# One DMA in place of two for three stores at the end of an attention and MLP kernel

## The chip, the cores and the metric

The kernel runs on one core of one Trainium2 chip. The metric is device time in microseconds; a run of the kernel before takes 364.1 us (median of three runs, 363.9 to 364.14). The names of the engines are those of the profile: PE is TensorE, PEld its weight loads, DVE is VectorE, ACT is ScalarE, POOL is GpSimd, SP is SyncE. SP, ACT and POOL also issue DMAs, each on a queue of its own; the core has 16 DMA engines, which do the moving.

## What is computed

Attention with a sigmoid in place of the softmax, and behind it a two-layer MLP with SiLU on all tokens:

```python
# q, k, v: (8, 12, 448, 64); w_in: (768, 2048); w_out: (2048, 768)
scores = q @ k.T / sqrt(64) - log(448)
attn_out = sigmoid(scores) @ v
x = attn_out.transpose(0, 2, 1, 3).reshape(3584, 768)
h = x @ w_in
out = (h * sigmoid(h)) @ w_out          # (3584, 768), float32
```

## The kernel before

The inputs are cast to 16 bits when they are loaded. Attention, the first matrix product (h) and the second (out) are interleaved by hand: generators issue a few TensorE instructions at a time, and an outer loop takes turns between them. The batches are handled in four pairs, m = 0 to 3. For m = 0 to 2 the out products of one pair run between the attention work of the next; for the last pair nothing is left to run between, so the kernel ends with a plain stretch of out products (the loop at L830).

The tokens of a batch are cut into 64 rows of 7 neighbours: token p * 7 + c belongs to chunk c (0 to 6), row p (0 to 63). `rows_of` (L490) is this view of the output: `rows_of[b, c]` is a piece of 64 rows of 768 floats, whose rows lie 7 output rows apart. Chunks c and c + 1 of one batch are neighbouring output rows. On chip, two chunks make up one block of 128 partitions: the first 64 partitions hold the one, the next 64 the other. `row_blocks(m, g)` (L518) gives the two output pieces that belong to block g of pair m; the 14 chunks of a pair make 7 blocks. Blocks 0 to 2 and 4 to 6 lie within one batch, block 3 takes the last chunk of one batch and the first of the next.

`out_set` (L521 to L580) computes two blocks at once. It uses seven products in place of eight, each of 8 matrix instructions into one PSUM bank (`product`, L535), with sums and differences on VectorE before and after. The results are two tiles `osb` of 128 x 768 floats, one for each block, and each has a left and a right half of 384 columns: c11 and c12 of the first, c21 and c22 of the second. In all sets but the last, each block is stored whole, as two DMAs of 64 rows by 3,072 bytes on SP. In the last set (`last=True`) each half is stored as soon as it is there, in pieces of 64 rows by 1,536 bytes:

- L556, after the second product: left half of the first block (c11), two DMAs on SP
- L567, after the fifth product: left half of the second block (c21), one on SP, one on ACT
- L572, after the sixth product: right half of the second block (c22), two on SP
- L577, after the seventh product: right half of the first block (c12), one on SP, one on ACT

The VectorE instructions that complete these halves are L553 (c11), L565 (c21), L570 (c22) and L575 (c12). The last set pairs block 6 of pair m = 2 with block 6 of pair m = 3: each is made of chunks 5 and 6 of one batch (L617 to L621). A queue issues its DMAs in the order of the program; the instruction that issues waits for the data by semaphore, and what stands behind it on that queue waits too.

Of the kernel before, what the change touches and what calls it, by code (L numbers as in the profile page):

```python
# [17 lines left out]
def kernel(  # L18
# [9 lines left out]
    nc = tc.nc  # L28
# [5 lines left out]
    HP = P // 2  # L34
    NCH = S // HP
# [53 lines left out]
    def one_bank(name):  # L89
        if "any" in banks:  # L90
            ring.append(ring.pop(0))
            return banks["any"].tile([P, 512], F32, tag=f"any{ring[-1]}", name=name)
        taken["single"] += 1
        return banks["single"].tile([P, 512], F32, tag="single", name=name)
# [395 lines left out]
    rows_of = out.rearrange("(b p c) e -> b c p e", b=B, c=NCH)  # L490
# [25 lines left out]
        return gTr[:, :, at : at + P]  # L516

    def row_blocks(m, g):  # L518
        return [rows_of[2 * m + u // NCH, u % NCH] for u in (2 * g, 2 * g + 1)]

    def out_set(a1, rows1, a2, rows2, last=False):  # L521
        lo, hi = slice(0, NHC), slice(NHC, NFC)
        osb = [p3.tile([P, DMODEL], F32, tag="osb", name="osb") for _ in range(2)]
        c11, c12 = (osb[0][:, nh * NO2 : (nh + 1) * NO2] for nh in range(2))
        c21, c22 = (osb[1][:, nh * NO2 : (nh + 1) * NO2] for nh in range(2))
        m1 = cpool.tile([P, NO2], F32, tag="m1", name="m1")
        sg = [cpool.tile([P, NHC, P], F16, tag=f"S{i}", name=f"S{i}") for i in range(1, 5)]

        def store(rows, o, cols, engines):
            for at, (row, eng) in enumerate(zip(rows, engines)):  # L530
                eng.dma_start(row[:, cols], o[at * HP : (at + 1) * HP, cols])

        left, right, whole = slice(0, NO2), slice(NO2, DMODEL), slice(0, DMODEL)

        def product(a, w):  # L535
            po = one_bank("po")
            for fc in range(NHC):
                nc.tensor.matmul(  # L538
                    po[:, :NO2], a[:, fc, :], w[:, fc, :], start=(fc == 0), stop=(fc == NHC - 1)
                )  # L540
                if fc < NHC - 1:
                    yield 163
            return po[:, :NO2]

        add, sub = nc.vector.tensor_add, nc.vector.tensor_sub
        add(sg[0], a2[:, lo], a2[:, hi])
        sub(sg[1], sg[0], a1[:, lo])
        po = yield from product(a1[:, lo], wq[0][0])
        (act_copy if last else nc.vector.tensor_copy)(m1, po)
        sub(sg[2], a1[:, lo], a2[:, lo])  # L550
        yield 163
        po = yield from product(a1[:, hi], wq[1][0])
        add(c11, po, m1)  # L553
        sub(sg[3], a1[:, hi], sg[1])
        if last:
            store(rows1, osb[0], left, (nc.sync, nc.sync))  # L556
        yield 163
        po = yield from product(sg[1], tw[2])
        add(c12, po, m1)
        yield 163  # L560
        po = yield from product(sg[2], tw[3])
        add(c22, po, c12)
        yield 163
        po = yield from product(a2[:, hi], tw[4])
        sub(c21, c22, po)  # L565
        if last:
            store(rows2, osb[1], left, (nc.sync, nc.scalar))  # L567
        yield 163
        po = yield from product(sg[0], tw[1])
        add(c22, po, c22)  # L570
        add(c12, po, c12)
        store(rows2, osb[1], right if last else whole, (nc.sync, nc.sync))  # L572
        yield 163
        po = yield from product(sg[3], wq[1][1])
        add(c12, po, c12)  # L575
        if last:
            store(rows1, osb[0], right, (nc.sync, nc.scalar))  # L577
        else:
            store(rows1, osb[0], whole, (nc.sync, nc.sync))
        yield 163  # L580
# [25 lines left out]
    def sets(m):  # L606
        for g in range(0, NCH - 1, 2):
            step = out_set(
                block(m, g), row_blocks(m, g), block(m, g + 1), row_blocks(m, g + 1)
            )  # L610
            for i, ns in enumerate(step):
                if m == 0 and g == 0 and i in (10, 14):
                    next(sums)
                if m == 0 and g == 0 and i in (20, 28, 36, 44):
                    next(in_sums)
                yield ns
        if m % 2 == 1:  # L617
            g = NCH - 1
            yield from out_set(
                kept, row_blocks(m - 1, g), block(m, g), row_blocks(m, g), m == B // 2 - 1  # L620
            )  # L621
# [240 lines left out]
```

## Time and profile before

| | |
|---|---|
| median of three runs | 364.1 us |
| the profiled execution, whole | 364.33 us |
| its span, first to last instruction | 362.3 us |
| PE busy | 355.9 us (98%) |
| DVE, ACT, POOL busy | 252.3, 249.0, 76.7 us |
| granted TensorE clock, mean | 0.999 |
| the last set's stores: SP, six DMAs of 96 KB | 2.2 us median from issue to landing |
| the last set's stores: ACT, two DMAs of 96 KB | 2.4 us |
| whole-block stores: SP, 52 DMAs of 192 KB | 3.1 us |

Times in the views are microseconds from the span's start unless marked ns. A line of the time line has the start, the length, the engine (with q: its queue, issuing), the line of the kernel, the operation, what it writes and reads, and the count; in brackets the idle time before it and what ended that. In the DMA views, one digit stands for one slice, the mean busy share of the 16 DMA engines in tenths, and below it what they moved in GB/s; q1 is the queue of SP and q10 that of ACT, each with its packets (rows and completion words), megabytes and share of 16 engines' time. DMA times are from the start of the issue to the last completion.

### The profile page before, as it was taken

The page shows a single profiled execution, that of the slowest core. Times are in us where ns is not written, and L with a number is a line of the kernel's source. Part 1 is how long each engine was busy: PE and PEld are TensorE (multiplying, and loading weights), DVE is VectorE, ACT ScalarE, POOL GpSimd, SP SyncE. Part 2 cuts the span into 40 slices and gives each one's busy share as a digit, 9 for nine tenths or more (in the row PEclk, how much of TensorE's full clock was granted, in tenths as well). Part 3 has the DMA queues.
Part 4 walks back from the last instruction along what each step waited for, and adds up shares of the span by engine and source line. Part 5 has one row for each costly group of instructions (what it writes and reads, how often), then busy time and mean ns, then how long its engine had stood idle before and what let it go on. Part 6 is the DMA issues. An engine that isn't in the chain of part 4 may idle for free.

```text
span 362.3 us, 7655 instructions
## 1 busy us (share of the span) xinstructions
PE 355.9 (98%) x3038; PEld 186.8 (52%) x3038; DVE 252.3 (70%) x461; ACT 249.0 (69%) x339; POOL 76.7 (21%) x115
## 2 busy tenths in 40 slices
PE   8999999999999999999999999999999999999995
PEld 5554445555555555555555545555455555556662
DVE  3665469777566587868566768795756677797763
ACT  5999886488999756688777846679889956640000
POOL 8666421040060262000033056000100000000000
PEclk9999999999999999999999999999999999999999
DMA  9999999979979599008679579901973120003333
GB/s 167 197 204 204 204 205 203 168 113 170 176 126 201 117 131 175 0 2 162 104 134 197 102 142 154 123 2 27 191 101 89 32 58 0 3 0 89 87 89 87
DMA packets 65860, 42.87 MB, mean 118 GB/s; under 512 B 35873, under 2 KB 62497, under 8 KB 65825
## 3 DMA queue, kind: packets, MB, share of 16 engines
q0 software_dynamic: 26800, 22.52, 43.1%
q1 hardware_dynamic: 38320, 19.34, 26.7%
q8 instruction: 24, 0.39, 0.4%
q10 hardware_dynamic: 704, 0.52, 0.4%
q14 instruction: 12, 0.09, 0.1%
HBM read 45.61 MB, written 11.01 MB: 156 GB/s over the span
## 4 chain that ended last, share of the span: by engine, by line
PE 96%; DVE 1%; DMA 1%; ACT 0%; issue 0%; DVEq 0%
PE po L538 37%; PE psc L259 11%; PE ph L322 10%; PE pav L290 9%; PE pa L412 8%; PE pd L412 8%; PE pc L412 8%; PE pb L412 4%; DMA qs<-in_q_dram 1%; PE ptrq L201 1%; DVE kT L208 1%; PE ptrk L201 1%; PE pw L188 0%; DVE xT L301 0%; ACT attnT L244 0%; DVE qT L208 0%
## 5 line engine op out<-in xcount | busy, mean ns | idle before, releaser
L266 ACT ACTIVATE attnT<-psc,bias_s 128x896 f16<-128x896 f32 x166 | 155.8, 1008 | 19.8 <-PE psc L259 18.3
L538 PEld LDWEIGHTS <-S 128*128 128x128 f16 x448 | 41.7, 98 | 34.1 <-issue 8.2
L259 PE MATMUL psc<-qT,kT 64*64 64x448 f16 x664 | 48.7, 361 | 0.9 <-ACT attnT L244 0.5
L301 DVE TENSOR_SCALAR xT<-pav 128x448 f16<-128x448 f32 x48 | 27.7, 619 | 29.0 <-PE pav L290 29.0
L538 PEld LDWEIGHTS <-gTr 128*128 128x128 f16 x336 | 31.7, 98 | 26.4 <-issue 6.6
L124 POOL DMA_DIRECT2D vf<-in_v_dram x24 | 17.3, 722 | 129.8 <-PE pav L290 106.7
L412 PEld LDWEIGHTS <-w_in_sb 128*128 128x128 f16 x288 | 27.9, 98 | 26.7 <-issue 1.1
L538 PE MATMUL po<-T,S 128*128 128x384 f16 x224 | 41.0, 327 | 0.0
L538 PE MATMUL po<-w_out_sb,gTr 128*128 128x384 f16 x224 | 41.0, 327 | 0.0
L538 PE MATMUL po<-w_out_sb,S 128*128 128x384 f16 x224 | 40.1, 327 | 0.0
L322 PE MATMUL ph<-xT,w_in_sb 128*128 128x448 f16 x192 | 38.5, 353 | 0.0
L290 PE MATMUL pav<-attnT,vf 64*64 64x448 f16 x672 | 38.1, 351 | 0.1
L412 PE MATMUL pa<-xT,w_in_sb 128*128 128x448 f16 x144 | 33.1, 353 | 0.0
L412 PEld LDWEIGHTS <-SI 128*128 128x128 f16 x216 | 21.1, 98 | 20.0 <-issue 0.5
L259 PEld LDWEIGHTS <-kT 64*64 64x64 f16 x664 | 17.1, 104 | 26.9 <-issue 20.7
L290 PEld LDWEIGHTS <-vf 64*64 64x64 f16 x672 | 21.7, 106 | 12.3 <-issue 2.9
L322 PEld LDWEIGHTS <-w_in_sb 128*128 128x128 f16 x192 | 17.8, 98 | 18.9 <-issue 3.5
L428 ACT ACTIVATE part<-pa 128x448 f32<-128x448 f32 x24 | 12.8, 541 | 17.7 <-PE pa L412 17.7
L406 ACT ACTIVATE gTr<-pc 128x448 f16<-128x448 f32 x24 | 13.0, 543 | 12.9 <-DVE pc L422 12.5
L538 PE MATMUL po<-T,gTr 128*128 128x384 f16 x112 | 21.5, 327 | 0.0
L422 DVE TENSOR_TENSOR part<-pb,part 128x448 f32<-128x448 f32 x24 | 14.9, 621 | 8.3 <-ACT part L428 5.0
L191 ACT ACTIVATE m<-po 128x384 f32<-128x384 f32 x1 | 0.5, 490 | 27.3 <-PE po L538 27.3
(80 smaller groups left out, 472.9 us busy)
## 6 DMA issues: line engine op xcount, KB each, us to landing
out_dram<-osb SPq DMA_DIRECT2D x52, 192.0 KB, 3.1
vf<-in_v_dram POOLq DMA_DIRECT2D x24, 224.0 KB, 6.4
kf<-in_k_dram POOLq DMA_DIRECT2D x23, 224.0 KB, 6.9
qf<-in_q_dram POOLq DMA_DIRECT2D x23, 224.0 KB, 7.8
w_in_sb<-in_moe_w_in_dram POOLq DMA_DIRECT2D x16, 192.0 KB, 8.0
w_out_sb<-in_moe_w_out_dram POOLq DMA_DIRECT2D x4, 768.0 KB, 15.1
out_dram<-osb SPq DMA_DIRECT2D x6, 96.0 KB, 2.2
kT<-kr SPq DMA_TRANSPOSE x18, 4.3
```

Source lines behind the costliest of these rows:

```text
L124: nc.gpsimd.dma_start(flat[name, g][:, :, c0:c1].rearrange("p i c d -> p i (c d)"), rows_in(name, g)[:, :, c0 * D : c1 * D],)
L201: nc.tensor.matmul(ptr[j * D : (j + 1) * D, (c - c0) * P : (c - c0 + 1) * P], flat[name, g][:, j, c, :], ident, start=True, stop=True,)
L259: nc.tensor.matmul(psc[own, j, :S], qkT["k", g][rows, ch, own], qkT["q", g][rows, :, own], start=True, stop=True,)
L266: nc.scalar.activation(attnT[g, ch], psc[:, :, :S], AF.Sigmoid, bias=bias_s, scale=QKSCALE)
L290: nc.tensor.matmul(pav[half][j * D : (j + 1) * D, :S], flat["v", g][own, j, ch, :], at[own, j, :], start=(ch == 0), stop=(ch == NCH - 1),)
L301: nc.vector.tensor_scalar_mul(xT[b][:, half * NQ + iq, :], pav[half][:, :S], SX)
L322: nc.tensor.matmul(ph[:, :S], w_in_sb[:, cc, fc * P : (fc + 1) * P], xT[b][:, cc, :], start=(at == 0), stop=(at == NCC - 1),)
L406: nc.scalar.activation(gTr[:, r * NG + i, col + c * S : col + (c + 1) * S], h, AF.Silu, bias=0.0, scale=ISX)
L412: nc.tensor.matmul(to, w[:, n, i * P : (i + 1) * P], x[:, n], start=(start and n == 0), skip_group_check=not start, stop=(n == NQ - 1),)
L422: nc.vector.tensor_add(o, po, x)
L428: nc.scalar.activation(got[i, 1], bank[i, "a"], AF.Copy)
L538: nc.tensor.matmul(po[:, :NO2], a[:, fc, :], w[:, fc, :], start=(fc == 0), stop=(fc == NHC - 1))
```

## The change

In the last set, three of the four pairs of stores become one DMA each, on SP: c11 (L556), c21 (L567, where one of the two was on ACT) and c22 (L572). The fourth, c12, stays as two DMAs on SP and ACT. `row_blocks` now gives one view of shape 2 x 64 x 768 where both chunks lie in one batch, and a list of two pieces otherwise; indexing it gives the same pieces as before, so the stores that stay are as they were. The source is the `osb` tile's 128 partitions. The bytes and where they go are the same; the line numbers after the diff are higher by up to 9.

```diff
     def row_blocks(m, g):
-        return [rows_of[2 * m + u // NCH, u % NCH] for u in (2 * g, 2 * g + 1)]
+        b, c = divmod(2 * g, NCH)
+        if c + 1 < NCH:
+            return rows_of[2 * m + b, c : c + 2]
+        return [rows_of[2 * m + b, c], rows_of[2 * m + b + 1, 0]]
...
         def store(rows, o, cols, engines):
-            for at, (row, eng) in enumerate(zip(rows, engines)):
-                eng.dma_start(row[:, cols], o[at * HP : (at + 1) * HP, cols])
+            if len(engines) == 1:
+                engines[0].dma_start(rows[:, :, cols], o[:, cols])
+                return
+            for at, eng in enumerate(engines):
+                eng.dma_start(rows[at][:, cols], o[at * HP : (at + 1) * HP, cols])
...
         if last:
-            store(rows1, osb[0], left, (nc.sync, nc.sync))
+            store(rows1, osb[0], left, (nc.sync,))
...
         if last:
-            store(rows2, osb[1], left, (nc.sync, nc.scalar))
+            store(rows2, osb[1], left, (nc.sync,))
...
-        store(rows2, osb[1], right if last else whole, (nc.sync, nc.sync))
+        if last:
+            store(rows2, osb[1], right, (nc.sync,))
+        else:
+            store(rows2, osb[1], whole, (nc.sync, nc.sync))
```

## The prediction

> **What bounds the kernel now.** I read the chain of waits first, then its last stretch in order of time, then the time line and the DMA views of the last 10 us. The whole page's chain:
>
> ```profile
> span 362.3 us, 7655 instructions
> PE 96%; DVE 1%; DMA 1%; ACT 0%; issue 0%; DVEq 0%
> ```
>
> TensorE sets the time until its last product. The change touches only what follows: how the last results leave. The chain from 350 us on (start, length, what) and, from the time line, the four VectorE results that release the last set's stores:
>
> ```profile
> 349.90 8.14 PE po L538 x50
> 358.04 0.02 issue
> 358.06 0.56 DVE osb L575
> ...
> 351.62 0.56 DVE L553 TENSOR_TENSOR osb<-po,m 128x384 f32<-128x384 f32 x1 [0.17 <-issue]
> 355.46 0.56 DVE L565 TENSOR_TENSOR osb<-osb,po 128x384 f32<-128x384 f32 x1 [0.74 <-PE po L538]
> 357.24 0.55 DVE L571 TENSOR_TENSOR osb<-po,osb 128x384 f32<-128x384 f32 x1
> 357.35 0.47 SPq L531 DMA_DIRECT2D out_dram<-osb  x1
> 358.65 0.50 ACTq L531 DMA_DIRECT2D out_dram<-osb  x1
> ```
>
> I call the stores A (L556, left half of the first block), B (L567), C (L572) and D (L577). The reader is to see that each is issued some 0.03 us after its result: A at 352.20 (351.62 + 0.56 and 0.03), B at 356.05, C at 357.35 (its data is ready at L570's end, 357.32), D at 358.65. D stays as it is, two DMAs of 64 rows on SP and ACT. Where the end lies, from the list of DMAs from 357.1 to 361.1 us:
>
> ```profile
> out_dram<-osb ACTq DMA_DIRECT2D x1, 96.0 KB, 2.4
> ```
>
> D on ACT is issued at 358.65 and lands 2.4 us later, at 361.05. The DMA engines move their last bytes shortly before 360.70 (their share after that is 0.00), so landing costs 0.35 us more. From 361.05 to the span's end lie 1.25 us of closing drains and semaphores, which go with the last landing. So the tail is: last landing + 1.25. A, B and C land earlier and cost nothing today.
>
> **Part 1: what goes.** Three issues, one for each of A, B and C (two on SP, one on ACT), about 0.5 us each of a queue. They hide: SP waits for results between the stores, and after its second issue for C (357.87 + 0.59 = 358.46) it is free before D's 358.65. Removing them is worth 0 for the end. On SP nothing is queued behind them but D, on ACT only D; no VectorE or TensorE instruction waits for A, B or C, since nothing overwrites these buffers.
>
> **Part 2: what comes.** Three stores of 128 rows of 1,536 B. In the built program the destination's steps read 2 x 64 x 384, the outer step being the block, where each old store reads 64 x 384. How rows are spread over the 16 DMA engines is what the case turns on, and the trace of before holds no store whose outer step counts 2. It shows this: a 64-row store makes 16 completion words beside its 64 rows, so four rows for each engine. And an issue takes as long for 256 pieces as for 64:
>
> ```profile
> L142 SPq DMA_DIRECT2D qs<-in_q_dram x1: 467/467/467, 0.7 to 0.7; - x1
> L531 SPq DMA_DIRECT2D out_dram<-osb x58: 466/584/885, 85.6 to 358.7; - x58
> ```
>
> The L142 load has 128 x 2 pieces, yet it costs the queue the same 467 ns as the cheapest 64-row store. The issuing side therefore does not deal out piece by piece; it cuts an access pattern by one of its steps. All plain transfers in the trace have an outer step of 64 or 128, which cuts into 16. Cut by the outer step, the merged stores give two engines 64 rows each, and 14 engines none. Bounds: 16 engines (8 rows each, no cost) and 2 engines. I take 2, because the outer step is the one that every row here is compatible with and the one whose cut needs no row count.
>
> The Trainium skill, "DMA: Bandwidth & Descriptors", section "Why a DMA increments its semaphore by 16 and not by 1", says that the engine count is the largest number up to 16 that divides the slowest non-unit step of both sides; here that is 2 (of 2 and 128), and the sum by it is the one below. No run here shows it yet.
>
> **The pace of one engine.** The trace has a stretch with one engine alone: it had been held up by a 16 KB instruction load and worked off its four rows of A after all others. The DMA view from 354.95 to 355.25 us, 40 slices of 7.5 ns (busy tenths and GB/s):
>
> ```profile
> DMA  0005000000050000000500000005000000000000
> GB/s 0 0 1 205 0 0 0 0 0 0 0 205 0 0 0 0 0 0 0 205 0 0 0 0 0 0 0 205 0 0 0 0 0 0 0 1 0 0 0 0
> ```
>
> Four rows, one each 8 slices: 0.060 us a row (25.6 GB/s). Completion words are under 0.01 us. The slower bound comes from the queues' shares with all engines at work, 358.4 to 360.8 us:
>
> ```profile
> q1 hardware_dynamic: 240, 0.30, 54.3%
> q10 hardware_dynamic: 80, 0.10, 11.5%
> ```
>
> q1 (SP): 54.3% x 16 x 2.4 us / 192 rows = 0.109 us a row. q10 (ACT): 11.5% x 16 x 2.4 / 64 = 0.069. I take 0.060, as the lone engine is nearest to two engines with a queue of their own.
>
> **The sum.** First bytes come 1.12 us after an issue: B's rows start near 357.17 for 356.05 (the DMA view from 357.1 us is empty for its first slices, then busy). So, on each of the two engines:
> - A: 353.33 + 64 x 0.060 = 357.17.
> - B: may start at 357.17, and does; until 361.01.
> - C: could start at 358.47, waits for B; until 364.85.
> - D: four rows from SP and four from ACT belong to these same two engines: 8 x 0.060, until 365.33; five completion words, 0.05: 365.38.
> - Landing 0.35: 365.73, against 361.05 today: **+4.7 us**.
>
> TensorE and VectorE are not moved; the whole cost lies behind the last product. The span becomes 362.3 + 4.7 = 367.0, the profiled time 364.33 + 4.7 = 369.0. The profiled run was 0.23 above the median of 364.1, so for a median I forecast **368.8**.
>
> **Rivals.**
> 1. *All 16 engines share the merged stores* (not slower). Each engine gets 8 rows a store, at most 0.87 us at 0.109; C is over by 359.4, before D's first rows at 359.77. D's result, issue and landing stay: **364.1**. For it: every transfer in the trace lands on 16 engines. Against it: none has an outer step below 16. The point from which it decides is a share that is done in the 1.30 us between C and D: 21 rows, so six engines or more. With four engines (32 rows, 1.92 us) B ends at 359.09, C at 361.01, D lands at 361.86: +0.8, **364.9**. A gain beyond 0.1 is excluded, as D waits for L575, which does not move. The same page of the Trainium skill advises, under "Rules for kernel authors", one 128-partition transfer in place of two on disjoint halves; by that advice this rival is the outcome. The trace shows only the two-halves form.
> 2. *Two engines, and the hand-over stalls as well.* When D is issued, each of the two engines has about 103 rows before it (39 of B, 64 of C). The largest load that the trace shows for one engine is a transpose's 896 pieces / 16 = 56. If D can be handed over only when C is done, it starts its 2.4 us near 364.85: landing 367.25, +6.2: **370.3**. With rows at q10's 0.069 as well (200 x 0.009 = 1.8) it is 372.1. If a 16 KB instruction load falls on one of the two engines, as it did on one engine here (about 1 us), it lies between these.
> 3. *Two engines at the loaded pace* of 0.109: 200 x 0.109 = 21.8 in place of 12.0: +14.5, **378.6**. Against it: 0.109 is measured where 16 engines work at once; with 14 idle, little is left to contend with.
>
> **Chances and range.** Forecast 0.68, rival 2 0.13, rival 3 0.05, rival 1 with 16 engines 0.12, with four to eight 0.02. A measurement of this kernel tells 0.2% (0.7 us) from no change. Two engines cost more than that in all forms (0.86), four engines just so (0.01): slower 0.87. The 16-engine case, and eight engines, give within 0.2% 0.11, faster 0.02. Low end: the highest rate in a 100 ns slice of the last 10 us is 430 GB/s, 0.057 us a row on each of 16 engines, which makes +4.1; with 0.6 for the spread of readings, 367.5. High end: rival 2 with slower rows, 372.5. That holds 0.81; rivals 1 and 3 stay outside.
>
> **What would show it.** SP's list has three stores of 192 KB. Right: A lands some 5.4 us after its issue (today about 3), B about 5.5, C about 8; between 353.4 and 365 us the DMA share is a flat 0.125 (2 of 16) at about 51 GB/s, at first beside TensorE, then alone for some 7 us after 358.6; the last VectorE result still ends near 358.6. Wrong: bursts of share above 0.5 within a microsecond of each store (rival 1), D's issue later than 358.7 or its first rows after C's last (rival 2), or about 28 GB/s in place of 51 (rival 3). If TensorE's last product moves, the account of the tail is wrong altogether.

## The result, and the profile after

The changed kernel takes 370.11 us (median of five runs, 369.97 to 370.2) against 363.99 us before: a ratio of 1.0165, 95% interval 1.0153 to 1.0176, so 6.1 us slower. The profiled execution took 370.11 us, its span is 368.2 us.

The chain's last stretch of the changed kernel, in order of time (start, length, what), and its last VectorE result and the issues of D in the time line:

```profile
348.87 8.95 PE po L544 x55
357.82 0.02 issue
357.84 0.56 DVE osb L584
...
358.43 0.52 SPq L537 DMA_DIRECT2D out_dram<-osb  x1
358.43 0.55 ACTq L537 DMA_DIRECT2D out_dram<-osb  x1
```

The reader is to see that nothing ahead of the stores became later: the last result and D's issue are even 0.22 us earlier than in the profile before, within what two executions differ by. All that was lost lies behind 358.4 us. The DMA view from 352 to 368 us, 40 slices of 0.4 us (busy tenths of 16 engines, GB/s), first of the kernel before, then of the changed one with its issues and the time from issue to landing:

```profile
DMA  9125581000000970758594000000000000000000
GB/s 353 46 41 127 119 196 31 19 0 0 0 0 23 200 265 4 169 123 188 127 238 138 0 0 0 0 0 0 0 0 20 0 0 0 0 0 0 0 0 0
...
DMA  6003111111111111111347941111111111110000
GB/s 254 0 0 72 38 35 19 42 31 50 50 50 50 50 50 50 50 54 46 58 73 138 254 146 58 46 50 31 38 50 42 42 46 54 50 50 35 12 0 0
...
out_dram<-osb SPq DMA_DIRECT2D x3, 192.0 KB
out_dram<-osb SPq DMA_DIRECT2D x1, 96.0 KB, 8.9
out_dram<-osb ACTq DMA_DIRECT2D x1, 96.0 KB, 5.5
```

Before, the stores are bursts with empty slices between them. Now it is a flat tenth from 353.2 to 366.8 us, at about 50 GB/s once it runs, broken only near 361 us, when D's rows arrive on the other engines. D itself, which the change left alone, lands 8.9 us (SP) and 5.5 us (ACT) after its issue in place of 2.2 and 2.4. No landing is printed for the three merged stores; the trace's completion words put A at 358.35 (6.4 us after its issue), B at 362.40 (6.6), C at 367.07 (9.9) and D at 367.32. How many engines are at work is seen in stretches (length, busy time of the engines, then the clock, the DMA share and GB/s); the last line is the list of packets for the second stretch:

```profile
353.20:355.50 2.30, 2.30 (x16) 1.37 (x14) 0.82 (x2) 0.00 (x0) 0.00 (x0) 1.00 0.16 39
355.50:359.80 4.30, 2.31 (x15) 1.18 (x12) 1.88 (x4) 0.00 (x0) 0.00 (x0) 1.00 0.13 50
363.60:367.00 3.40, 0.00 (x0) 0.00 (x0) 0.00 (x0) 0.00 (x0) 0.00 (x0) 0.50 0.12 45
...
DMA packets 142, 0.22 MB, mean 50 GB/s; under 512 B 2, under 2 KB 142, under 8 KB 142
```

A share of 0.125 is two engines of 16. The first stretch holds a 16 KB instruction load as well (0.96 us of one engine), and is slower than the pace that follows; more on that below. Of the 142 packets from 355.50 to 359.80 us two are completion words (under 512 B): the store A, 128 rows, ends with two words, where a 64-row store before made 16.

Not all of D waits for the end of the line. On the two engines SP's rows of D come last, behind C. ACT's rows come between C's rows: the queues from 362.3 to 363.7 us are

```profile
q1 hardware_dynamic: 30, 0.05, 8.7%
q10 hardware_dynamic: 10, 0.01, 4.7%
```

The ten packets of q10 are ACT's four rows for each of the two engines and their two words, beside 28 rows of C and two words on q1. ACT's half of D has landed at 363.95, 3.1 us before C.

### The profile page after: what moved, and what is told of

The parts are those of the page before. It is cut to its first block, busy times and chain, and to the rows that moved or that the text cites. A ratio compares the mean times of both kernels' runs of the same rounds, so it can differ in the third digit from the quotient of the medians.

```text
span 368.2 us, 7651 instructions
## 1 busy us (share of the span) xinstructions
PE 355.5 (97%) x3038; PEld 186.7 (51%) x3038; DVE 252.3 (69%) x461; ACT 249.2 (68%) x339; POOL 76.8 (21%) x115
## 4 chain that ended last, share of the span: by engine, by line
PE 95%; DVE 2%; issue 0%; ACT 0%; DVEq 0%
PE po L544 36%; PE psc L259 11%; PE ph L322 10%; PE pav L290 9%; PE pa L412 7%; PE pd L412 7%; PE pc L412 7%; PE pb L412 4%; PE pw L188 1%; DVE kT L208 1%; PE ptrq L201 1%; PE ptrk L201 1%; DVE xT L301 0%; DVE qT L208 0%; DVE osb L584 0%
## 5 line engine op out<-in xcount | busy, mean ns | idle before, releaser
L422 DVE TENSOR_TENSOR part<-pc,part 128x448 f32<-128x448 f32 x24 | 15.0, 623 | 6.1 <-PE pc L412 5.5
```

The source lines that it names most:

```text
L422: nc.vector.tensor_add(o, po, x)
```

## The experiments

The theory: the outer step of 2 puts a merged store on two engines, and the three stores and their share of D form one line there. The times of before beside the runs were 363.81 (first four kernels), 363.97 (next four) and 364.04 us (last three); each ratio is against its own.

**C alone.** A and B are issued in two, as before; C stays merged.

```diff
-            store(rows1, osb[0], left, (nc.sync,))
+            store(rows1, osb[0], left, (nc.sync, nc.sync))
...
-            store(rows2, osb[1], left, (nc.sync,))
+            store(rows2, osb[1], left, (nc.sync, nc.scalar))
```

> Only C (right half of the second block) is one DMA; A and B are two each, as before. Theory (the outer step of 2 puts a merged store on two engines, 0.061 us a row, in one line with D's rows): C's rows run from about 358.5 for 3.9 us, up to 0.8 us more if its first rows come slowly as A's did, then D's eight rows 0.5 and the landing 0.35: last landing 363.3 to 364.0 in place of 361.05, so 366.2 to 367.0 us. Rival 1 (the loss comes of three merged stores following each other, one alone is absorbed): 364.0. Rival 2 (each merged store costs a fixed third of the 6.1 us): 366.0, which this run alone does not tell from the theory; the run with A alone does.

Measured: 366.99 us, ratio 1.0086 (1.0071 to 1.0101), +3.2 us. This is the theory's upper end, and 1.0 above rival 2. Stretches of this run: C's start, D's arrival, the end:

```profile
358.38:360.50 2.12, 0.00 (x0) 0.00 (x0) 0.06 (x1) 0.00 (x0) 0.00 (x0) 1.00 0.13 33
362.10:363.70 1.60, 0.00 (x0) 0.00 (x0) 0.00 (x0) 0.00 (x0) 0.00 (x0) 0.50 0.13 48
```

Two engines' share both times, but 33 GB/s at first and 48 later. So rival 1 (one merged store alone is absorbed) falls.

**A alone.** B and C are issued in two; A stays merged.

```diff
-            store(rows2, osb[1], left, (nc.sync,))
+            store(rows2, osb[1], left, (nc.sync, nc.scalar))
...
-            store(rows2, osb[1], right, (nc.sync,))
+            store(rows2, osb[1], right, (nc.sync, nc.sync))
```

> Only A (left half of the first block) is one DMA; B and C are two each. Theory: A is on two engines until about 358.0 and lands some 6.4 us after its issue; B's share of these two engines is late by up to 1 us, C and D are not: 364.0 us, within 0.3. Rival 2 (each merged store costs a fixed third): 366.0.

Measured: 363.82 us, ratio 1.0001 (0.9991 to 1.001). A lands at 358.04, 6.4 us after its issue, just as in the changed kernel, and costs nothing: the last store lands 2.5 us later, at 360.51. A fixed cost for each merged store (rival 2) is ruled out. What counts is how far the line on the two engines reaches past D.

**The same merging with an outer step of 64.** The two blocks' tokens are reordered by copies on the idle ACT before the last set (32 in the trace, 0.31 us each, not 64 as the expectation says), so that partition 2p + c holds row p of chunk c; all four stores, D too, are one DMA.

```diff
+            act_copy(
+                t[:, f].rearrange("k (h c p) -> k h c p", c=2, h=64),
+                a[:, f].rearrange("k (c h p) -> k h c p", c=2, h=64),
+            )
...
-                engines[0].dma_start(rows[:, :, cols], o[:, cols])
+                engines[0].dma_start(rows[:, :, cols].rearrange("c p e -> p c e"), o[:, cols])
...
-            store(rows1, osb[0], right, (nc.sync, nc.scalar))
+            store(rows1, osb[0], right, (nc.sync,))
```

> All four stores of the last set, D too, are one DMA of 128 rows on SP, but the block's tokens are reordered beforehand (64 small copies on the idle ACT during the last stretch) so that the destination's steps read 64 x 2 x 384: the same rows, bytes and neighbours in memory, with an outer step of 64. Theory: 16 engines with 8 rows each, landing some 2.3 to 2.8 us after the issue; the end moves by -0.3 to +0.2: 363.7 to 364.2 us. Rival 3 (a store of 128 rows in two steps is slow by itself, by its scattered rows or its longer pattern): 370 us or more, since D is merged as well.

Measured: 363.36 us, ratio 0.9986 (0.9976 to 0.9995), 0.3 below the theory's range; more on that at the end of this section. The DMA view of this run from 356 to 361 us, slices of 0.125 us, and its issues:

```profile
DMA  0000029998100001898930000059995000000000
GB/s 0 0 0 0 0 86 369 381 381 307 49 0 0 0 0 61 319 381 319 369 123 0 0 0 0 0 221 393 369 369 209 12 0 0 0 0 0 0 0 0
...
out_dram<-osb SPq DMA_DIRECT2D x3, 192.0 KB, 2.2
```

The same 128 rows of the same bytes to the same places, written with steps of 64 x 2 x 384 in place of 2 x 64 x 384: three short bursts on all engines, each landing 2.2 us after its issue, where the changed kernel took 6.4 to 9.9. Neither the row count, the scattered rows nor the three-step pattern is slow by itself. This is the run that decides for the outer step.

**Outer steps of 4 and 8.** Here the stores are those of the kernel before, eight DMAs of 64 rows, and only the way in which the destination's steps are written differs. A first attempt wrote the 64 rows as 4 x 16 in their order:

```diff
-                eng.dma_start(row[:, cols], o[at * HP : (at + 1) * HP, cols])
+                dst = row[:, cols]
+                if last:
+                    dst = dst.rearrange("(h p) e -> h p e", h=4)
+                eng.dma_start(dst, o[at * HP : (at + 1) * HP, cols])
```

> The kernel before, with eight DMAs of 64 rows; see the next line for the pattern. Theory: an outer step of 4 that cannot be merged puts each on four engines with 16 rows.

Measured: 363.77 us, ratio 1.0 (0.999 to 1.0009). It tried nothing: the two steps fit into one and were merged into 64 x 384 when the program was built; in the trace the destination reads 64 rows and each DMA still makes 16 completion words. It only shows that the pattern has to be looked up as the instruction carries it. With steps that don't merge ("(p h) e -> h p e"; the rows of a store then stand in another order within its own places):

> The kernel before, with its eight DMAs of 64 rows at the end, but each destination is written as 4 x 16 x 384 with steps that cannot be merged (outer step 7 output rows, inner step 28): the 64 rows of a store go to that store's own 64 places in another order, so rows of the last two blocks are permuted in the output. Same DMAs, bytes and places. Theory: four engines with 16 rows for each DMA, so 32 rows for each pair: B from 357.2 to 359.1, C to 361.1, D to 363.0, landing 363.4 against 361.05: +2.3, up to +3.1 with a slow start as A's: 366.1 to 366.9 us on 363.8. Rival 3 (three steps in the pattern are slow, whatever the outer count): +6 or more, as with 2. Rival 4 (it is the bytes or rows of one DMA that count, not the outer step): 363.8.

Measured: 368.33 us, ratio 1.0117 (1.0092 to 1.0141), +4.4 us.

> The same with 8 x 8 x 384 (outer step 7 output rows, inner 56); rows of the last two blocks are permuted in the output. Theory: eight engines with 8 rows for each DMA; a pair's 16 rows take 1.0 us, less than the 1.3 us between the stores; D's last rows end near 360.8: within 0.4 us of before, 363.8 to 364.2. Rival 3: +6 or more. Rival 4: 363.8, so this run tells only the theory and rival 3 apart, and with the run with 4 the point from which the spread decides.

Measured: 364.79 us, ratio 1.0024 (1.0008 to 1.0039), +0.8 us. In the trace each DMA makes 4 completion words in the first run and 8 in the second. Stretches of the run with 4 from B's first rows on, then of the run with 8:

```profile
357.10:361.50 4.40, 0.82 (x6) 0.29 (x3) 1.14 (x3) 0.00 (x0) 0.00 (x0) 0.97 0.25 70
362.50:364.50 2.00, 0.00 (x0) 0.00 (x0) 0.00 (x0) 0.00 (x0) 0.00 (x0) 0.50 0.25 94
```

```profile
358.30:360.80 2.50, 0.00 (x0) 0.00 (x0) 0.14 (x1) 0.00 (x0) 0.00 (x0) 0.92 0.47 139
```

Shares of 0.25 and 0.47: four engines, and just under eight. The engine count follows the outer step, so rival 4 falls, and with the run with 8, +0.8 us at the same number of steps, rival 3 falls too. Both sizes miss the theory's line of rows, by 1.3 us or more and by 0.4. The run with 4 shows why in part: 70 GB/s at first, and the second DMA of B (ACT) has its first rows at 358.64, 2.7 us after its issue; before, ACT's rows came 1.56 us after. That issue alone held ACT's queue for 1.38 us (1.45 with an outer step of 8), before 0.55. Why is not known.

**All four at an outer step of 2.** As the changed kernel, with D merged too (`(nc.sync, nc.scalar)` becomes `(nc.sync,)`).

> As the changed kernel, with D merged too (2 x 64 x 384). Theory: the two engines have 4 x 64 rows in one line; against the changed kernel D's share is 64 rows in place of 8: +56 x 0.061 = 3.4 us, less up to 0.7 that D's rows from two queues lost there: 372.6 to 373.3 us (base 363.8). Rival 1 (the loss is not a line of rows): 370 to 372.

Measured: 373.04 us, ratio 1.0239 (1.0217 to 1.0262), inside the theory's range. Its line of 4 x 64 rows an engine:

```profile
353.38:355.70 2.32, 2.32 (x16) 1.37 (x14) 0.84 (x2) 0.00 (x0) 0.00 (x0) 1.00 0.13 32
355.70:369.90 14.20, 2.28 (x15) 1.17 (x12) 1.85 (x4) 0.00 (x0) 0.00 (x0) 0.70 0.13 50
```

After a slow start of 2.3 us it holds 50 GB/s to the end: 25 GB/s an engine, 0.061 us a row.

**Half the bytes for C.** As the run with C alone, but C stores 192 of its 384 columns (`slice(NO2, NO2 + NO2 // 2)`); the rest is left out.

> As the run with C alone merged, but C stores only its first 192 columns (768 bytes a row); the other 192 columns of the right half of the second block are left out. The open question is why a merged store that starts on idle engines loses 0.8 us in its first 24 rows for each engine. If its rows are handed over slowly at first (theory 2), C's first 24 rows again take about 2.3 us and D's rows start as late as with full rows (1.5 us or more after D's issue); the whole ends some 0.5 to 1.3 us earlier than with full rows: 365.7 to 366.5 us. If the DMA engines themselves are slow at first with rows of 1,536 bytes, half the bytes take half the time: C is over after 2.4 us and the time is 364.3 to 365.0 us.

Measured: 364.79 us, ratio 1.0024 (1.001 to 1.0037), +0.75 us, inside the range of the second reading. C's first 24 rows an engine (48 packets):

```profile
358.30:359.18 0.88, 0.00 (x0) 0.00 (x0) 0.06 (x1) 0.00 (x0) 0.00 (x0) 1.00 0.13 42
```

They take 0.88 us in place of 2.3, and the 64 rows 2.5 us in place of some 5. Theory 2, a hand-over that is slow by the row, falls. The second reading, half the time for half the bytes, holds for the whole store but not for its start, which takes well under half: with short rows the slow start is nearly gone. In the slow stretches above, too, the engines count as busy all the time (0.13) while they move only 33 GB/s. Why rows of 1,536 bytes last up to 0.33 us there is not settled: it happens where a two-engine store starts on idle engines (A in the changed kernel and alone, C alone), and not where it follows another (B). Idle engines alone are not enough for it: the stores with an outer step of 64 start on idle engines too, and their rows last some 0.066 us from the first on.

**Where the gain of the reordered kernel lies.** The kernel with an outer step of 64, with D again in two DMAs (32 x 2 x 384, on SP and ACT), twice, the second time beside the one with D merged:

```diff
-            store(rows1, osb[0], right, (nc.sync,))
+            store_halves(rows1, osb[0], right, (nc.sync, nc.scalar))
```

> As the run with the reordered tokens and outer step 64, but D is two DMAs of 32 x 2 x 384 on SP and ACT again; A, B and C stay one each. If the 0.45 us gained there come from D's rows being handed over at once (today ACT's rows follow SP's by 0.44 us), the gain is lost here: 363.7 to 363.9 us. If they come from A, B and C being merged, or from the reordering, it stays: 363.3 to 363.5.

> The variant with D in two DMAs on SP and ACT, on the same chip as the one with D merged. If D's single hand-over is the gain: slower than that one by 0.3 to 0.5 us and equal to before. If the gain is in A, B and C or in the reordering: equal to that one.

> The kernel with reordered tokens, all four stores merged at an outer step of 64, again beside its variant with D in two: 363.3 to 363.6 us on a base of 363.9, faster than before by 0.3 to 0.5 us.

Measured: 363.74 us, ratio 0.9987 (0.9974 to 1.0), then 363.72 us, ratio 0.9994 (0.9986 to 1.0003), beside 363.62 us, ratio 0.9994 (0.9985 to 1.0002), for the one with D merged. By these times the two can't be told apart, and the second time neither could be told from before; a gain of some 0.1% is under the 0.2% that a measurement of this kernel tells from no change. The ends of the traces say more. From D's last issue to the end of the span the kernel before takes 3.66 us, the one with D merged 3.20 in both its traces, the one with D in two 3.45 in both. Of both gains some 0.3 us is in the closing: when the last store has landed, SP has seven waits for DMA semaphores before it in the kernel before, and two in these (more on that below). The other part is the landing, 2.38 us after the issue before, 2.21 with D merged and 2.46 with D in two. So D's single hand-over is worth some 0.25 us and the closing 0.3, in the traces; no version tried here clearly beats the kernel before by its measured times.

## Why the prediction was right, and where its size was off

**What bounds the kernel**: right. The last product and result did not move; all of the loss is behind them.

**Part 1, what goes is worth nothing**: right for the issues themselves. With an outer step of 64 the same three issues are gone, and D still waits for its data. What I left out is the closing: the program deals its DMA semaphores to the stores in turn, so with three stores fewer D signals others, and the closing after the last landing takes 0.92 us in place of 1.28.

**Part 2, two engines**: right, and shown by two completion words, a share of 0.13 and the runs with 4, 8 and 64. The trace before could not show it; the argument from equal issue times (467 ns for 256 and for 64 pieces) only said that the cut is by a step and not by the piece. The rule of the Trainium skill ("DMA: Bandwidth & Descriptors", "Why a DMA increments its semaphore by 16 and not by 1") gives 2, 4, 8 and 16 engines for these patterns, and the traces agree with each. The Trainium skill's other rule on the same page ("Rules for kernel authors": one 128-partition transfer in place of two halves) holds in the run with an outer step of 64, where 192 KB land in 2.2 us like 96 KB before. With an outer step of 2 it costs 6.1 us.

**The sum**: the right work on the right engines, 1.3 us short in the median (370.1 against 368.8 forecast, inside the range of 367.5 to 372.5). By its own terms, from A's issue on, in us:

| term | forecast | measured |
|---|---|---|
| issue to A's first rows | 1.12 | 1.22 |
| A's 64 rows | 3.84 | 4.77 |
| B's 64 rows | 3.84 | 3.96 |
| C's 64, D's 8 rows, words | 4.37 | 5.05 |
| landing | 0.35 | 0.34 |
| closing | 1.25 | 0.92 |

The term that is off most is A's 64 rows x 0.060. The pace of 0.060 from the lone engine's four rows is right for a line that is running (0.061), but A's first 24 rows an engine took 2.3 us in place of 1.5. C and D cost 0.7 more than forecast; in that stretch three of ACT's rows of D lasted 0.18 to 0.29 us. The closing was some 0.3 shorter than I took it for, which by luck hides a part of the shortfall. SP waits there for the DMA semaphores one after another in a fixed order, 0.06 us each once they are all done. Its waits after the last landing, before and in the changed kernel:

```profile
L857 SPq EVENT_SEMAPHORE  x7: 28/28/28, 361.1 to 361.4; - x7
L866 SPq EVENT_SEMAPHORE  x1: 28/28/28, 367.3 to 367.3; - x1
```

Before, the last landing is that of an early semaphore in this order; now it is that of the last one. The order in the sum was wrong at one point: ACT's four rows did not stand behind C but came between its rows. That changes little in the sum, since the two engines have the same rows to move either way.

**Rivals.** Rival 1 (16 engines) did not happen, but it is what the outer step of 64 gives. Its limit of 0.1 for a gain left out the closing. Its point of decision, six engines or more, was not tried: the run with eight cost 0.8 us, but there D too is on eight engines. Rival 2 (the hand-over, the passing of a DMA's rows to the engines, stalls as well) gives 370.3; by the time alone it would be the better match. The trace decides: D's first rows came 1.44 us after its issue in place of 1.12, ACT's 2.47 after in place of 1.56 (2.06 in the run with C alone), so there was a stall in small part, but nothing waited until C was done. (Its largest load of 56 pieces an engine overlooks the w_out loads: 4,096 pieces in four DMAs, 64 an engine if 16 share them.) Rival 3 (0.109 us a row throughout) did not happen.

## What to carry to other kernels

When two transfers are joined into one, look at the outer step as the instruction carries it: here the destination's, and not the number of rows or bytes, decided how many of the 16 DMA engines worked. The source's outer step was 64 or 128 in all runs, so nothing is shown for that side. A small factor such as 2 for "two blocks" has to be an inner step, with the 64 or 128 rows outside. A poorly spread transfer was free where it was over before the last one was issued (A alone). Otherwise its rows stand in line before the share of every later transfer of the same queue on these engines, and they delay the share of another queue too, whose rows come between them.

## What was not expected of the hardware

- A store that starts on two idle engines begins slowly: its first 24 rows an engine take 2.3 us at 32 GB/s, with the engines counted as busy, before 50 GB/s are reached. With rows of 768 bytes the first 24 take 0.88 us.
- A 128-row store at an outer step of 64 moves its 192 KB in about 0.7 us at up to 393 GB/s, and its rows last some 0.066 us; SP's 64-row stores of the kernel before needed 0.6 to 0.7 us for half of that, at 0.109 us a row.
- A share of D on the crowded engines is late on either queue: ACT's half landed 5.5 us after its issue though its queue held nothing else.
